# Routed attention and a feed-forward layer on one core: a second batch in cluster order, its outcome fetched by halves

## The chip, the cores and the metric

One core of a Trainium2 chip runs the whole program. The metric is the device time of one execution in microseconds, the median of three runs. A profile of one execution, taken by the hardware profiler, gives the times of single instructions.

## The reference

```python
# q, k, v: (4, 8, 768, 64); centroids: (8, 16, 64); w_in 512x2048, w_out 2048x512
q_assign = argmax(normalised(q) . normalised(centroids))      # 16 clusters per head
k_assign = argmax(normalised(k) . normalised(centroids))
mask = q_assign[:, :, :, None] == k_assign[:, :, None, :]
scores = where(mask, q @ k.T / 8, -1e9)
attn = softmax(scores) @ v                                     # (B, H, S, D)
x = attn as (B*S, H*D) = (3072, 512)
h = x @ w_in
out = (maximum(h, 0) + alpha * minimum(h, 0)) @ w_out
```

A query attends only to keys of its own cluster. Everything is in fp32.

## The kernel before

**Attention.** There are 4 batches with 4 *pairs* of heads each; a tile holds both heads of a pair, 64 partitions each. The first `WHOLE` batches (3 before) are done *whole*: for each half of the queries (384) all six chunks of 128 keys are scored on TensorE (`score`, L757), exponentiated on ScalarE (L778, L775), masked on VectorE by comparing cluster numbers (`mask`, L798; batch 0 is masked in the product instead), summed up (`add_up`, L808; `turn`, L827; `rows_sums`, L835), inverted and spread (`invert`, L861; `spread_out`, L868), weighed with v (`weigh`, L893) and normalised into `xT` (`normalise`, L993).

The other batches go in *cluster order*. `order_features` (L564), `order_sims` (L573), `order_counts`, `order_begins` (L598), `order_ranks`, `order_rows` (L619) and `order_clusters` find for each token its row in the order of clusters. `order_stage` (L652, SP) loads a third of a head's q, k and v (256 tokens) into one of two stage tiles; `order_scatter` (L663, POOL) sends 64 of these tokens to their rows in DRAM by an indirect DMA, four for each stage. These stand in the list `sorting`, 24 scatters and 6 stages a pair. Later `order_load` (L674, L683, L692, 12 DMAs on SP) fetches the ordered pair; `order_blocks` (L699) and `order_queries` (L705) on VectorE prepare it. As neighbours in order are of equal or neighbouring clusters, a chunk of keys is scored against at most three chunks of queries (`window`): 2048 columns a head where a whole pair has 4608. `add_near`, `weigh_near` (L926) and `normalise_near` (L932) end it. Then `to_rows` (L955, L958) turns the outcome to rows, `put_back` (L963, POOL) sends it by 12 indirect DMAs to the tokens' rows in DRAM, `fetch_back` (L975, SP) reads it in token order and `turn_back` (L985, VectorE) transposes it into `xT`.

**Feed-forward layer.** `ffn_pieces` makes 28 pieces for each half of a batch: 16 `hidden` (L1017, copied on ScalarE, sloped on VectorE, L1009) and 12 `final` (L1035). The last batch goes by `last_pieces` (L1195, L1251), a scheme with fewer products on halves of x and w.

**Order.** The order is written by hand (`manual_schedule`). Time is counted in steps; three steps (15 ticks, 12 of them slots) are one half of a whole pair or one ordered pair, and 12 steps one block (`UB`). A block does attention, and between it feeds pieces of the layer for the block before; `kept(block)` pieces are left for the next. `load_at` and `prep_at` hold what starts at a step; `later(ticks, piece)` defers; `ORDERS` holds the steps in which an ordered pair's raw tiles are loaded. `steps` lists the whole batches and then the ordered ones:

```python
steps += [(n, None, s) for n in range(NO, NP) for s in range(SB)]
```

Every engine runs its own instructions in this order. POOL's queue holds scatters and put-backs, SP's queue every plain load and store. Buffers by pool: `inp` 4 (raw q and k, outcome before and after it is put back), `vpool` 4, `xpool` 2 (`xT`), stage tiles 2.

Of the kernel before, what the change touches and what calls it, by code (L numbers as in the profile page):

```python
# [23 lines left out]
def kernel(  # L24
# [19 lines left out]
    HJ = NJ // 2  # L44
    HS = HJ * P
    SCALE = float(D) ** -0.5
    WHOLE = 3

    GROUP = 2
    assert D == 64 and S % (2 * P) == 0 and HS <= 512 and DM == H * D and H * NC == P  # L50
# [60 lines left out]
    def load(n):  # L111

        b, hp = pairs[n]
        for w, src in enumerate((q, k)):
            raw = inp.tile([P, 2, NJ, D], FP32, name="qk")
            if n < NCH:
                nc.sync.dma_start(
                    out=raw.rearrange("p h j d -> p h (j d)"),  # L120
                    in_=src[b, 2 * hp:2 * hp + 2].rearrange("h (p j) d -> p h (j d)",
                                                            j=NJ))
            for h in range(2):
                rows = src[b, 2 * hp + h]
# [367 lines left out]
    def second_part():  # L492

        first_part.close()
        for name, bufs in (("emore", 1), ("ordc", 1), ("ordp", 1), ("order", NP - NO),
                           ("xmore", 1), ("byrow", 1)):
            sorts[name] = fast.enter_context(tc.tile_pool(name=name, bufs=bufs))
        for i in range(5):
            e_tiles.insert(0, sorts["emore"].tile([P, 2, HS], FP32, name=f"more{i}"))
# [78 lines left out]
    def order_counts(n, ps):  # L578

        top, first, pieces = argmax(ps, exact=True)  # L580
        member = sorts["ordp"].tile([P, HS], BF16, name="mine")
        pieces.append(lambda: nc.vector.transpose(
            out=member, in_=top.rearrange("p t c -> p (t c)")))

        def scan():
            count = asg.tile([P, HS], FP32, name="simT")
            nc.vector.tensor_tensor_scan(count, member, member, 0.0, ALU.add, ALU.max)
            us[n] = member, count
        pieces.append(scan)
# [339 lines left out]
    def normalise_near(n):  # L929
        outT = inp.tile([P, 2, NJ, D], FP32, name="qk").rearrange("p h j d -> p (h j d)")  # L930
        for side in range(2):
            nc.vector.tensor_tensor(out=outT[:, side * HS:(side + 1) * HS],  # L932
                                    in0=pos.pop((n, side))[:, 0:HS],
                                    in1=rds.pop((n, side)), op=ALU.mult)
        whole = tc.dram_tile([2 * S, D], FP32, name=f"back{n}")
        to = dram_disjoint_views(whole, 2 * NJ)
        found = orders.pop(n)
        place = sorts["order"].tile([P, 2, NJ], I32, name="place")
        nc.vector.tensor_scalar(out=place, in0=found[:, :, :, 0], scalar1=0, scalar2=S - 1,
                                op0=ALU.max, op1=ALU.min)  # L940
        rows = sorts["byrow"].tile([P, NJ, P], FP32, name="rows")

        starts = (6, 9)
        for i in range(2):
            later(starts[i], lambda i=i: to_rows(outT, rows, i))
            for x in range(NJ):
                later(starts[i] + 2 + x // 2,
                      lambda i=i, x=x: put_back(to, place, rows, i * NJ + x))
        later(starts[1] + 2 + HJ, lambda: fetch_back(n, whole))

    def to_rows(outT, rows, i):

# [12 lines left out]
            out_offset=bass.IndirectOffsetOnAxis(ap=place[:, h, j:j + 1], axis=0),  # L965
            in_=rows[:, j, h * D:(h + 1) * D], in_offset=None, element_offset=h * S * D)

    def fetch_back(n, whole):

        b, hp = pairs[n]  # L970
        raw = inp.tile([P, 2, NJ, D], FP32, name="qk").rearrange("p h j d -> p (h j d)")
        for h in range(2):
            for x in range(D // Q):
                r = h * D + x * Q
                nc.sync.dma_start(  # L975
                    out=raw[r:r + Q, :].rearrange("p (t i) -> p t i", i=Q),
                    in_=whole[h * S:(h + 1) * S, x * Q:(x + 1) * Q].rearrange(
                        "(t p) i -> p t i", p=Q))

        def turn_back():  # L980
            for half in range(2):
                if (b, half) not in xTs:
                    pool = sorts["xmore"] if half else xpool
                    xTs[b, half] = pool.tile([P, NCH, HS], FP32, name="xT")
                nc.vector.transpose(out=xTs[b, half][:, hp, :],  # L985
                                    in_=raw[:, half * HS:(half + 1) * HS])
        later(4 if n == NP - 1 else 9, turn_back)

    def normalise(n, half):
        b, hp = pairs[n]  # L990
        if (b, half) not in xTs:
            xTs[b, half] = xpool.tile([P, NCH, HS], FP32, name="xT")
        nc.vector.tensor_tensor(out=xTs[b, half][:, hp, :],  # L993
                                in0=pos.pop((n, half))[:, 0:HS],
                                in1=rds.pop((n, half)), op=ALU.mult)

# [83 lines left out]
            nc.vector.tensor_tensor(out=to, in0=x, in1=y, op=op)  # L1080

    def sum_x(which):
        x0, x1 = (xTs[B - 1, half] for half in range(2))
# [5 lines left out]
        B11, B21, B12, B22 = (x0[:, 0:KH], x0[:, KH:NCH], x1[:, 0:KH], x1[:, KH:NCH])  # L1089
        for to, x, y in ((T1, B12, B11), (T2, B22, T1), (B12, B22, B12), (T4, B21, T2))[which]:  # L1090
            nc.vector.tensor_tensor(out=to, in0=x, in1=y, op=ALU.subtract)

    def last_pieces():
# [93 lines left out]
        def hidden(x):  # L1187
# [12 lines left out]
            def x_of(half, kh):  # L1200
                return xTs[b, half][:, kh * KH:(kh + 1) * KH]

            def g_of(f, half):
                return g[f][0][half]
# [1 line left out]
            def p1():  # L1206
                if not g:
                    places()
                copy(g_of(f1, 0), product("a", "11", x_of(0, 0), True))

            def p5():
                copy(g_of(f2, 1), product("e", "S1", x_sums[0], True))

            def p2():
                plus(g_of(f1, 0), product("z", "12", x_of(0, 1), True))
                if late:
                    late.popleft()()

# [1 line left out]
                copy(g_of(f1, 1), product("a", "S2", x_sums[1], False))  # L1220

            def p3():
                plus(g_of(f1, 1), product("e", "S4", x_of(1, 1), False))
                slopes(f1)

            def p7():
                plus(g_of(f2, 1), product("a", "S3", x_of(1, 0), False))
                late.append(p4)
                if x % 2 == 0 and x:
                    g_sums(x - 2)  # L1230
# [508 lines left out]
```

## Time and profile before

| | before |
|---|---|
| median of 3 runs | 968.09 us (967.7 to 968.3) |
| the profiled execution: device time / span | 968.97 / 967.2 us |
| PE (products) busy | 946.1 us, 98% |
| VectorE (DVE) busy | 683.5 us, 71% |
| ScalarE (ACT) busy | 260.0 us, 27% |
| GpSimd (POOL) busy | 213.2 us, 22% |
| TensorE clock granted | 1.0 throughout |
| 16 DMA engines busy (queue of SP) | 25.6% |

By stages (us from the start of the span; busy times of the engines in it):

| stretch | length | PE | DVE | ACT | POOL | what |
|---|---|---|---|---|---|---|
| 221 to 341 | 120 | 119.4 | 87.5 | 27.9 | 17.6 | batch 1, first half whole |
| 341 to 461 | 120 | 120.0 | 89.9 | 28.1 | 37.0 | batch 1, second half whole |
| 461 to 581 | 120 | 120.0 | 91.3 | 27.7 | 17.4 | batch 2, first half whole |
| 581 to 693 | 112 | 110.9 | 84.9 | 27.2 | 37.9 | batch 2, second half whole |
| 693 to 806 | 113 | 106.7 | 77.6 | 25.6 | 47.7 | batch 3 in cluster order |

How to read it: an instruction of an engine that works in order starts when the one before it has ended and its operands are there. An engine that is idle costs time only if what it does next is waited for by the chain that ends last. DMA-issuing instructions on POOL count as busy for the time POOL takes over them, not for the transfer.

### The profile page before, as it was taken

How to read it: one execution, taken by the hardware profiler on the slowest of the kernel's cores; microseconds unless marked ns; L12 is line 12 of the kernel's file. 1: busy time of each engine (PE TensorE's matmuls, PEld its weight loads, DVE VectorE, ACT ScalarE, POOL GpSimd, SP SyncE). 2: the span in 40 equal slices, each digit the busy share in tenths (PEclk: the TensorE clock that was granted, in tenths of full speed). 3: DMA queues.
4: the chain of work that ended last, by engine and by line, in shares of the span. 5: the costliest groups of instructions: out<-in, count | busy, mean ns of one | idle time of the engine just before them, and what ended most of it. 6: DMA issues, size and time to landing. Idle time of an engine off the chain costs nothing.

```text
span 967.2 us, 11202 instructions
## 1 busy us (share of the span) xinstructions
PE 946.1 (98%) x4059; PEld 502.8 (52%) x4059; DVE 683.5 (71%) x1241; ACT 260.0 (27%) x474; POOL 213.2 (22%) x249
## 2 busy tenths in 40 slices
PE   8999999999999999999999999999998999999997
PEld 5534444445454454544545445454454454556886
DVE  5897788798587776977868777678888735598200
ACT  5764533323121231222312223222222210121000
POOL 1432222110000645401000065550043541000000
PEclk9999999999999999999999999999999999999999
DMA  8433666053200463416020031450621112000000
GB/s 290 141 113 102 143 136 118 17 114 88 55 1 22 127 134 70 87 28 123 1 33 1 25 89 50 94 103 11 88 49 30 33 32 56 1 1 0 21 24 25
DMA packets 175583, 64.67 MB, mean 67 GB/s; under 512 B 161360, under 2 KB 165152, under 8 KB 175520
## 3 DMA queue, kind: packets, MB, share of 16 engines
q1 hardware_dynamic: 170064, 55.62, 25.6%
q0 software_dynamic: 4608, 7.87, 2.5%
q8 instruction: 34, 0.56, 0.2%
q10 hardware_dynamic: 848, 0.39, 0.2%
q14 instruction: 29, 0.24, 0.1%
HBM read 45.15 MB, written 18.35 MB: 66 GB/s over the span
## 4 chain that ended last, share of the span: by engine, by line
PE 92%; DVE 5%; issue 1%; ACT 1%; POOL 0%; DVEq 0%; ACTq 0%; POOLq 0%
PE fps L1035 25%; PE fps L1017 25%; PE vps L893 9%; PE sps L757 8%; PE sps L1251 4%; PE sps L1195 4%; PE fps L757 3%; PE vps L1251 2%; PE vps L1195 2%; PE fps L1251 1%; PE fps L1195 1%; PE mps L381 1%; PE mps L926 1%; PE vps L926 1%; PE sps L766 1%
## 5 line engine op out<-in xcount | busy, mean ns | idle before, releaser
L1017 PE MATMUL fps<-xT,w_in_sb 128*128 128x384 f32 x768 | 259.2, 491 | 0.0
L1035 PE MATMUL fps<-w_out_sb,gT 128*128 128x512 f32 x576 | 256.0, 597 | 1.1 <-DVE gT L1009 1.1
L1017 PEld LDWEIGHTS fps<-xT,w_in_sb 128*128 128x128 f32 x768 | 142.3, 190 | 103.9 <-ACT more L778 4.4
L663 POOL DMA_INDIRECT scratch<-stage,off x96 | 102.0, 1063 | 324.8 <-DMA stage<-in_v_dram 269.7
L1035 PEld LDWEIGHTS fps<-w_out_sb,gT 128*128 128x128 f32 x576 | 106.9, 190 | 127.2 <-issue 117.9
L1023 ACT COPY gT<-fps 128x384 f32<-128x384 f32 x96 | 45.9, 478 | 225.0 <-PE fps L1017 212.5
L798 DVE SCALAR_TENSOR_TENSOR more<-aq,key,more 128x384 f32<-128x384 bf16 (+1 forms) x136 | 74.5, 606 | 35.1 <-ACT more L778 20.0
L757 PE MATMUL sps<-qkT 64*128 64x384 f32 (+1 forms) x512 | 97.4, 494 | 0.1
L1009 DVE SCALAR_TENSOR_TENSOR gT<-gT,alpha 128x384 f32<-128x384 f32 x96 | 61.3, 646 | 33.2 <-ACT gT L1023 24.0
L778 ACT ACTIVATE E<-sps 128x768 f32<-128x768 f32 (+1 forms) x81 | 61.0, 801 | 73.2 <-PE sps L766 38.4
L963 POOL DMA_INDIRECT back<-rows,place x48 | 47.7, 994 | 105.1 <-ACT rows L958 91.7
L757 PEld LDWEIGHTS sps<-qkT 64*128 64x128 f32 x512 | 46.3, 186 | 45.0 <-issue 18.1
L798 DVE SCALAR_TENSOR_TENSOR E<-aq,key,E 128x384 f32<-128x384 bf16 (+1 forms) x104 | 56.6, 601 | 17.2 <-ACT E L778 11.3
L893 PE MATMUL vps<-E,vt 128*64 128x384 f32 x356 | 65.7, 494 | 1.5 <-DVE xT L993 1.5
L808 DVE TENSOR_TENSOR acc<-acc,E 128x768 f32<-128x768 f32 x47 | 44.9, 955 | 14.9 <-ACT E L778 13.6
L778 ACT ACTIVATE more<-sps 128x768 f32<-128x768 f32 (+1 forms) x47 | 35.6, 796 | 49.6 <-PE fps L1035 21.6
L893 PEld LDWEIGHTS vps<-E,vt 128*64 128x64 f32 x356 | 23.0, 136 | 33.4 <-issue 31.0
L271 POOL TENSOR_TENSOR w_in_sb<-w_in_sb,power 128x512 f32<-128x512 f32 x16 | 24.3, 1520 | 71.2 <-DVE w_in_sb L268 71.2
L893 PE MATMUL vps<-more,vt 128*64 128x384 f32 x220 | 38.8, 491 | 0.0
L1041 ACT COPY y<-fps 128x512 f32<-128x512 f32 x18 | 10.5, 586 | 100.8 <-PE fps L1035 81.6
L757 PE MATMUL fps<-qkT 64*128 64x384 f32 x160 | 34.9, 508 | 0.6 <-ACT more L775 0.6
L271 POOL TENSOR_TENSOR w_out_sb<-w_out_sb,power 128x512 f32<-128x512 f32 x16 | 22.5, 1410 | 55.8 <-DVE w_out_sb L268 55.8
(282 smaller groups left out, 1074.4 us busy)
## 6 DMA issues: line engine op xcount, KB each, us to landing
raw<-in_moe_w_in_dram SPq DMA_DIRECT2D x16, 512.0 KB
raw<-in_moe_w_out_dram SPq DMA_DIRECT2D x16, 512.0 KB
out_dram<-y SPq DMA_DIRECT2D x21, 256.0 KB
vt<-in_v_dram SPq DMA_DIRECT2D x12, 384.0 KB
qk<-in_q_dram SPq DMA_DIRECT2D x48, 96.0 KB
qk<-in_k_dram SPq DMA_DIRECT2D x48, 96.0 KB
w_in_kept<-w_in_sb SPq DMA_DIRECT2D x8, 512.0 KB
qk<-scratch SPq DMA_DIRECT2D x32, 96.0 KB
```

The costliest lines, as they stand in the source:

```text
L271: nc.gpsimd.tensor_tensor(out=dst, in0=dst, in1=power[0].bitcast(FP32), op=ALU.mult)
L663: nc.gpsimd.indirect_dma_start(out=scratch[n][1][h * NX + xx], out_offset=bass.IndirectOffsetOnAxis(ap=ranks[n][:, xx, h:h + 1], axis=0), ...
L757: nc.tensor.matmul(out=bank(ps, h, m), lhsT=qkT[r:r + D, S + c * P:S + (c + 1) * P], rhs=qkT[r:r + D, tokens], start=True, stop=not early_ ...
L778: nc.scalar.activation(out=E[:, :, 0:m], in_=ps[:, :, 0:m], func=AF.Exp, scale=SCALE)
L798: nc.vector.scalar_tensor_tensor(out=e, in0=of, scalar=keys[n][:, NJ + c, h:h + 1], in1=e, op0=ALU.is_equal, op1=ALU.mult)
L893: nc.tensor.matmul(out=po[r:r + D, 0:HS], lhsT=vts[n][:, h, c, :], rhs=e[:, h, :], start=(c == 0), stop=(c == NJ - 1))
L963: nc.gpsimd.indirect_dma_start(out=to[i], out_offset=bass.IndirectOffsetOnAxis(ap=place[:, h, j:j + 1], axis=0), in_=rows[:, j, h * D:(h + ...
L1009: nc.vector.scalar_tensor_tensor(out=gs[f], in0=gs[f], scalar=alpha[:, f:f + 1], in1=gs[f], op0=ALU.mult, op1=ALU.max)
L1017: nc.tensor.matmul(out=ps[:, 0:HS], lhsT=w_in_sb[:, c, f * P:(f + 1) * P], rhs=xTs[b, half][:, c, :], start=(c == 0), stop=(c == NCH - 1))
L1035: nc.tensor.matmul(out=ps[:, 0:DM], lhsT=gs[f][:, i * P:(i + 1) * P], rhs=w_out_sb[:, f, :], start=on and f == f0, stop=off and f == f0 + ...
L1195: nc.tensor.matmul(out=bank[to], lhsT=w_in_form(m, x, cc), rhs=rhs[:, cc, :], start=start and cc == 0, stop=cc == KH - 1, skip_group_check ...
L1251: nc.tensor.matmul(out=bank[to], lhsT=g_form(m, x, t), rhs=w_out_form(n, x), start=start and x == 0, stop=x == NQ - 1, skip_group_check=no ...
```

## The change

Batch 2 joins batch 3 in cluster order (`WHOLE = 2`), so there are 8 ordered pairs in place of 4 and 72 steps in place of 84. All eight are ordered by steps 26 to about 57, in and after batch 1; up to two entries of `sorting` a slot are done in place of one. The features are transposed in place, and their raw tiles come from a pool of their own with two buffers, `inp2`. `order_begins` follows its counts by ticks instead of at a step.

The outcome of an ordered pair of batch 2 comes back by halves of its tokens: the first half at the tick at which the whole came back so far, the second half (`inp2`) in steps 62 to 65. Batch 3 comes back behind the last block, whole. The second half of the last batch's x lies in two tiles of `inp2` (`x_last`) and no longer in a pool `xmore`. `kept` leaves 2, 4, 12 and 34 pieces after blocks 2 to 5 (before: 4 and 12 after blocks 5 and 6).

```diff
-    WHOLE = 3
+    WHOLE = 2
...
-            raw = inp.tile([P, 2, NJ, D], FP32, name="qk")
+            raw = (inp if n < NO else sorts["inp2"]).tile([P, 2, NJ, D], FP32, name="qk")
...
-        for name, bufs in (("emore", 1), ("ordc", 1), ("ordp", 1), ("order", NP - NO),
-                           ("xmore", 1), ("byrow", 1)):
+        for name, bufs in (("emore", 1), ("ordc", 1), ("ordp", 1), ("order", 5),
+                           ("inp2", 2), ("byrow", 1)):
...
     def order_features(n, w):
-        us[n, w] = inp.tile([P, 2, NJ, D], FP32, name="qk").rearrange("p h j d -> p (h j d)")
-        nc.vector.transpose(out=us[n, w],
-                            in_=raw_qk.pop((n, w)).rearrange("p h j d -> p (h j d)"))
+        us[n, w] = raw_qk.pop((n, w)).rearrange("p h j d -> p (h j d)")
+        nc.vector.transpose(out=us[n, w], in_=us[n, w])
...
+        later(len(pieces) + 3, lambda: order_begins(n))
...
-        later(starts[1] + 2 + HJ, lambda: fetch_back(n, whole))
+        backs[n] = whole
+        if pairs[n][0] < B - 1:
+            later(starts[1] + 2 + HJ, lambda: fetch_back(n, (0,)))
+        elif n == NP - 1:
+            for i in range(NCH):
+                later((1, 4, 7, starts[1] + 2 + HJ)[i],
+                      lambda i=i: fetch_back(NP - NCH + i, (0, 1)))
...
-    def fetch_back(n, whole):
+    backs, x_last = {}, []
+
+    def fetch_back(n, halves):
 
         b, hp = pairs[n]
-        raw = inp.tile([P, 2, NJ, D], FP32, name="qk").rearrange("p h j d -> p (h j d)")
+        whole = backs[n]
+        t0, t1 = halves[0] * HS, (halves[-1] + 1) * HS
+        raw = (sorts["inp2"] if halves == (1,) else inp).tile(
+            [P, 2, NJ, D], FP32, name="qk").rearrange("p h j d -> p (h j d)")
         for h in range(2):
             for x in range(D // Q):
                 r = h * D + x * Q
                 nc.sync.dma_start(
-                    out=raw[r:r + Q, :].rearrange("p (t i) -> p t i", i=Q),
-                    in_=whole[h * S:(h + 1) * S, x * Q:(x + 1) * Q].rearrange(
+                    out=raw[r:r + Q, t0:t1].rearrange("p (t i) -> p t i", i=Q),
+                    in_=whole[h * S + t0:h * S + t1, x * Q:(x + 1) * Q].rearrange(
                         "(t p) i -> p t i", p=Q))
 
         def turn_back():
-            for half in range(2):
-                if (b, half) not in xTs:
-                    pool = sorts["xmore"] if half else xpool
-                    xTs[b, half] = pool.tile([P, NCH, HS], FP32, name="xT")
-                nc.vector.transpose(out=xTs[b, half][:, hp, :],
+            for half in halves:
+                nc.vector.transpose(out=x_of(b, half, hp),
                                     in_=raw[:, half * HS:(half + 1) * HS])
         later(4 if n == NP - 1 else 9, turn_back)
 
+    def x_of(b, half, hp):
+        if (b, half) == (B - 1, 1):
+            if not x_last:
+                x_last.extend(sorts["inp2"].tile([P, 2, NJ, D], FP32, name="qk").rearrange(
+                    "p h j d -> p (h j d)").rearrange("p (c q) -> p c q", q=HS)
+                    for _ in range(2))
+            return x_last[hp // 2][:, hp % 2, :]
+        if (b, half) not in xTs:
+            xTs[b, half] = xpool.tile([P, NCH, HS], FP32, name="xT")
+        return xTs[b, half][:, hp, :]
...
-    ORDERS = [27, 33, 51, 57]
+    ORDERS = [26, 29, 33, 36, 40, 43, 46, 49]
...
-                at(t + 2, 2 + 2 * i, lambda n=n, i=i: order_features(n, i))
+                at(t + 2, 2 + i, lambda n=n, i=i: order_features(n, i))
...
-            at(t + 7, 2, lambda n=n: order_begins(n))
...
-            for i, p in ((5, 0), (7, 1)):
+            for i, p in ((-7, 0), (-5, 1)):
...
-        return {NS // UB - 2: 4, NS // UB - 1: 12}.get(block, 0)
+        return {2: 2, 3: 4, 4: 12, 5: 34}.get(block, 0)
...
+    for i in range(NCH):
+        load_at.setdefault(NS - UB + 2 + i, []).append(
+            lambda i=i: fetch_back(NO + i, (1,)))
...
-        if u == ORDERS[0] - 2:
+        if u == TOGETHER + 1:
             order_constants()
...
-            if sorting:
+            for _ in range(min(2, len(sorting))):
                 sorting.popleft()()
```

The products of the last batch read `x_last` in place of `xTs[B - 1, 1]`, with no other change.

More of the change, by code (lines that the diff above doesn't have):

```diff
@@ L975, in fetch_back @@
                 nc.sync.dma_start(
-                    out=raw[r:r + Q, :].rearrange("p (t i) -> p t i", i=Q),
-                    in_=whole[h * S:(h + 1) * S, x * Q:(x + 1) * Q].rearrange(
+                    out=raw[r:r + Q, t0:t1].rearrange("p (t i) -> p t i", i=Q),
+                    in_=whole[h * S + t0:h * S + t1, x * Q:(x + 1) * Q].rearrange(
                         "(t p) i -> p t i", p=Q))
         def turn_back():
-            for half in range(2):
-                if (b, half) not in xTs:
-                    pool = sorts["xmore"] if half else xpool
-                    xTs[b, half] = pool.tile([P, NCH, HS], FP32, name="xT")
-                nc.vector.transpose(out=xTs[b, half][:, hp, :],
+            for half in halves:
+                nc.vector.transpose(out=x_of(b, half, hp),
                                     in_=raw[:, half * HS:(half + 1) * HS])
         later(4 if n == NP - 1 else 9, turn_back)
+    def x_of(b, half, hp):
[8 more added lines that the diff above has]
+        return xTs[b, half][:, hp, :]
     def normalise(n, half):
         b, hp = pairs[n]
-        if (b, half) not in xTs:
-            xTs[b, half] = xpool.tile([P, NCH, HS], FP32, name="xT")
-        nc.vector.tensor_tensor(out=xTs[b, half][:, hp, :],
+        nc.vector.tensor_tensor(out=x_of(b, half, hp),
                                 in0=pos.pop((n, half))[:, 0:HS],
@@ L1082, in sum_x @@
     def sum_x(which):
-        x0, x1 = (xTs[B - 1, half] for half in range(2))
+        x0 = xTs[B - 1, 0]
         if not x_sums:
@@ L1088, in sum_x @@
         T1, T2, T4 = x_sums
-        B11, B21, B12, B22 = (x0[:, 0:KH], x0[:, KH:NCH], x1[:, 0:KH], x1[:, KH:NCH])
+        B11, B21, B12, B22 = (x0[:, 0:KH], x0[:, KH:NCH], *x_last)
         for to, x, y in ((T1, B12, B11), (T2, B22, T1), (B12, B22, B12), (T4, B21, T2))[which]:
@@ L1198, in product, with x_part @@
                 return bank[to]
-            def x_of(half, kh):
-                return xTs[b, half][:, kh * KH:(kh + 1) * KH]
+            def x_part(half, kh):
+                return x_last[kh] if half else xTs[b, 0][:, kh * KH:(kh + 1) * KH]
             def g_of(f, half):
@@ L1208, in p1 @@
                     places()
-                copy(g_of(f1, 0), product("a", "11", x_of(0, 0), True))
+                copy(g_of(f1, 0), product("a", "11", x_part(0, 0), True))
             def p5():
@@ L1214, in p2 @@
             def p2():
-                plus(g_of(f1, 0), product("z", "12", x_of(0, 1), True))
+                plus(g_of(f1, 0), product("z", "12", x_part(0, 1), True))
                 if late:
@@ L1222, in p3 @@
             def p3():
-                plus(g_of(f1, 1), product("e", "S4", x_of(1, 1), False))
+                plus(g_of(f1, 1), product("e", "S4", x_part(1, 1), False))
                 slopes(f1)
             def p7():
-                plus(g_of(f2, 1), product("a", "S3", x_of(1, 0), False))
+                plus(g_of(f2, 1), product("a", "S3", x_part(1, 0), False))
                 late.append(p4)
```

## Prediction

> **What bounds the kernel now.** I read the page's totals, the chain, the windows by stage, and then the timelines of POOL and SP, because the change gives work to those two. The page, engines' totals and POOL's line of the 40 slices:
>
> ```profile
> PE 946.1 (98%) x4059; PEld 502.8 (52%) x4059; DVE 683.5 (71%) x1241; ACT 260.0 (27%) x474; POOL 213.2 (22%) x249
> POOL 1432222110000645401000065550043541000000
> ```
>
> PE has 98% of the span; POOL's mean of 22% hides slices at 6 tenths. The chain that ended last, four pieces (start, us, what, instructions):
>
> ```profile
> 673.59 4.02 PE vps L893 x24
> ...
> 698.37 1.88 PE vps L926 x16
> 700.25 1.73 PE mps L926 x16
> ...
> 722.27 1.88 PE vps L926 x16
> ```
>
> The weighing of one *half* of a whole pair costs 4.02 us, that of a *whole* cluster-ordered pair 1.88 + 1.73 = 3.61 us. The windows (length, then PE, PEld, DVE, ACT, POOL busy, clock, DMA, GB/s):
>
> ```profile
> 461.00:581.00 120.00, 120.00 (x460) 59.12 (x459) 91.33 (x160) 27.65 (x52) 17.40 (x20) 1.00 0.13 30
> ...
> 698.00:722.00 24.00, 22.10 (x112) 12.66 (x108) 22.46 (x41) 6.96 (x15) 8.75 (x9) 1.00 0.38 62
> 722.00:754.60 32.60, 29.16 (x116) 14.63 (x114) 21.72 (x39) 7.33 (x14) 14.52 (x15) 1.00 0.12 29
> ```
>
> In a whole-pair block PE never rests and DVE has 76%. In the cluster-ordered block PE already loses 1.9 and 3.4 us in two pairs, and DVE has 22.46 of 24 us. POOL's timeline (start, us, line, operation, idle before and releaser):
>
> ```profile
> 370.57 0.96 POOL L663 DMA_INDIRECT scratch<-stage,off  x1 [0.30 <-issue]
> 371.84 0.96 POOL L663 DMA_INDIRECT scratch<-stage,off  x1 [0.31 <-issue]
> ...
> 630.98 1.02 POOL L663 DMA_INDIRECT scratch<-stage,off  x1 [6.14 <-DMA stage<-in_v_dram]
> ...
> 749.96 0.95 POOL L963 DMA_INDIRECT back<-rows,place  x1 [0.30 <-issue]
> 751.21 0.96 POOL L963 DMA_INDIRECT back<-rows,place  x1 [0.30 <-issue]
> ```
>
> From one start to the next a scatter (L663) takes 1.27 us, a put-back (L963) 1.27 us; the copy between scatters with its gap (374.07 to 374.54) takes 0.48. The 6.14 us are SP's doing:
>
> ```profile
> 618.47 6.17 SPq L683 DMA_DIRECT2D qk<-scratch  x8
> ```
>
> Here SP issued the loads of an ordered pair one after the other, and POOL's next stage stood behind them.
>
> **What the change removes.** Call a stretch the three steps of one score set: 1a0 to 1a3 and 1b0 to 1b3 for the two halves of batch 1, 2.0 to 2.3 and 3.0 to 3.3 for the ordered pairs. Per pair of batch 2, PE loses 8.04 - 3.61 = 4.43 us of weighing. The scores go from 4608 to 2048 columns a head; at the same 4.02 us for 12 products of 384 columns that is 8.04 x (1 - 2048/4608) = 4.47. It gains six transposes (L955, 4.1 us for four pairs, so 1.0) and two one-column products (0.2), and loses one denominator product (0.1). Net -7.8 a pair, -31.4 for four. Four stretches fewer save some 0.65 us each of small gaps (full stretches last that much longer than the sum of their products): -2.6. The 6 us that PE idled between 698 and 774 go into the account of what comes next. The span without any new wait would be 967.2 - 31.4 - 2.6 - 6 = 927.
>
> **What it adds.** Scatters go from 96 to 192, put-backs from 48 to 96, stage loads from 72 to 144, ordered loads from four pairs to eight. As the program is built, all 192 scatters stand between the end of 1a2 and the end of 3.0, and the put-backs of 2.0 to 2.3 stand in 2.1, 2.2, 2.3 and 3.0, between scatters, on the same queue. Counting instructions by the rows' durations (us; POOL = 1.27 per DMA + 0.48 per copy):
>
> | stretch | 1a3 | 1b0 | 1b1 | 1b2 | 1b3 | 2.0 | 2.1 | 2.2 | 2.3 | 3.0 | sum |
> |---|---|---|---|---|---|---|---|---|---|---|---|
> | PE | 29.8 | 26.0 | 33.1 | 23.9 | 29.0 | 25.1 | 22.3 | 27.6 | 20.6 | 30.9 | 268 |
> | DVE | 29.6 | 26.3 | 27.4 | 27.1 | 34.4 | 31.6 | 35.2 | 29.1 | 22.7 | 27.0 | 290 |
> | POOL | 27.8 | 25.3 | 26.5 | 26.0 | 27.8 | 27.8 | 40.5 | 41.8 | 41.3 | 37.5 | 322 |
>
> For example 2.1 on POOL: 18 scatters and 12 put-backs, 30 x 1.27, and 5 copies. DVE's 35.2 there is a near pair's 21 us (masks 6.8, sums, turns, blocks), some 10 us of one pair's ordering (L564 0.95 twice, argmax chain 3.1, scan 0.93, ranks, begins) and slopes. PE's work shrinks, and that of the two engines beside it grows in the same place.
>
> **Who waits for POOL.** The outcome of pair 2.k is put back in the next stretch; `fetch_back` on SP waits for its twelfth put-back (all rows may lie in either half); `turn_back` on DVE stands 9 ticks later, 40% into the stretch after, and DVE runs in order, so behind it queue masks, sums and slopes, and PE behind those. And xT of batch 2, half 0, is needed at about the same place: twelve pieces of batch 1 (36 us) are kept to cover it, and stretches 3.0 and 3.1 eat them. So POOL's 322 us must be over by 40% into 3.1. PE alone would be there 268 + 10 x 0.65 + 0.4 x 36 = 289 us after the start of 1a3.
>
> **The sum.** 1a3 begins at 290.2 in the profile, about 289 after the change (1a1 and 1a2 together are 1.7 shorter on PE). Up to the end of 1b1 POOL is paced by PE (90.9 with gaps): 380. In 1b2, 1b3 and 2.0 POOL's 81.6 exceeds PE's 78, and three ordered loads each hold SP. The two such places before cost POOL 6.14 and 1.97 us; I take 4 each: 94, so 474. In 2.1 to 3.0 POOL has 161 against PE's 101; the put-backs between scatters give the stage loads time, 4 for waits: 639. Then completion 1.5 (a scatter ended at 374.1, SP went on at 375.6), four issues 2.4 and landing 2: 645 for the last turn. PE's remaining work: 0.6 of 3.1 (21), 3.2 (37), and 3.3 with the tail, which is counted at 281 and, by the gap between count and trace in the tail before (205.6 counted, 214.7 lasted), lasts 290. That is 645 + 21 + 37 + 290 = 993. Add 1.8, which lay around the span in the profiled execution (968.97 against 967.2); the median lay 0.9 below that execution: 994. The loss is 67 us of waiting against 40 saved.
>
> Unknown are POOL's pace under doubled traffic and SP's waits. Lower bound: POOL never waits from the start of 1a3, 1.27 each: 289 + 322 + 6 + 348 = 965, median 966. Upper: each DMA at the mean of all (scatter 1.06 + 0.30, put-back 0.99 + 0.30, copy 0.34 + 0.28), which makes 1b2 to 3.0 260 instead of 243, and 6 us for each of six ordered loads: 380 + 260 + 36 + 6 + 348 = 1030. I lean to the lower pace, because it is the median of the scatters from 560 to 650 (0.98).
>
> The edits with one answer: the features are transposed in place and the raw tiles come from a pool of two (no work moved; a load waits for the ordering before it, 3 steps earlier); up to two sorting pieces a slot are counted above. The second halves of batch 2 come back from the end of 3.0 on and batch 3 behind the last block; 34 kept pieces, some 100 us of PE, cover that, where 12 did. If that cover failed it would cost some 10 us (one fetch and one turn).
>
> **The skill against the rows.** The Trainium skill, "Perfetto Trace Analysis", Identifying the Most-Contended Engine, would have the engine of highest occupancy optimised first; that is PE, and the sum would be the 927 above. The page allows for regimes with other engines in front, and the rows by stretch show one. "DMA: Bandwidth & Descriptors", Anatomy of one DMA — SWDGE (gpsimd) path, puts a fixed 2.0 us on each such DMA, mostly completion. As POOL's own time that would make an estimated 472 us of 236 DMAs and a span over 1100; the rows' 1.27 from start to start speak against reading it so.
>
> **Rivals.** *DVE alone binds (faster).* If POOL's lateness is taken up, because put-backs land earlier than I place them or PE runs on while DVE waits, what remains is DVE's excess: from 1b2 to 2.3 it has 180 us against PE's 152 with gaps, 28, some 32 with its own idle: 927 + 32 = 959, 960 as a median. For it: DVE waited only once for a fetched outcome before ("4.3 us" of L985). Against: that was with POOL at 15 us a stretch, not 41. It decides if POOL's wall time from 1a3 to the last put-back stays under some 315 us; the sum of its rows is 322.
> *POOL and SP hold each other up (still slower).* Stage loads, ordered loads and fetches share SP's queue in order, and there are only two stages: 6 us at every ordered load and the slower pace give 1010 to 1030. For it: the 6.14 us row. Against: put-backs between scatters leave the loads time.
> *Nothing to measure.* POOL at its lower bound gives 966, by chance beside 968.
>
> **How the numbers follow.** POOL sets the end with moderate waits (975 to 1010): 0.64, my forecast, 994. POOL and SP together, over 1010: 0.24. Near the lower bound, within 0.2% (966.2 to 970, about what a measurement of this kernel can tell from no change): 0.04. Faster: 0.08, the DVE rival. The range leaves out the faster case and the top of the SP case: 969 to 1020.
>
> **What would show it.** Right: POOL over 85% busy from about 380 to 640; PE idle for 60 us or more, in 1b3 to 3.1; DVE's `turn_back` (L985, after the change L993) waiting tens of us for DMA of back; SP's fetch waiting for put-backs; PE busy down to some 915. Wrong: `turn_back` waits under 10 us in all, or POOL shows gaps in 2.1 to 3.0 and PE none; then the time is below 960. If PE's idle time lies before masks while POOL has rest, DVE was the bound.

## The result and the profile after

| | before | after |
|---|---|---|
| median | 968.11 us (4 runs, 967.7 to 968.3) | 1073.78 us (4 runs, 1066.0 to 1079.9) |
| profiled execution: device time / span | 968.97 / 967.2 us | 1066.01 / 1064.2 us |
| PE idle, 290 to 760 (before: 290 to 806) | 7.4 us | 90.5 us |
| granted clock, mean | 1.0 | 0.946 |

The ratio of the medians is 1.109, with a 95% interval of 1.101 to 1.117. The loss is 106 us where 26 were forecast, and the time lies outside the range.

Page after the change, engines' totals, POOL's line and the clock's line of the 40 slices:

```profile
PE 955.7 (90%) x3931; PEld 507.3 (48%) x3931; DVE 659.8 (62%) x1229; ACT 246.0 (23%) x450; POOL 363.2 (34%) x417
POOL 2342222000271746666764756524425100000000
PEclk9999999999999899999868777989999999999999
```

PE executes 128 products fewer (3931 against 4059), and yet is busy 10 us longer, because several of the slices in which POOL works have a clock of 6 to 8 tenths. POOL itself is not full there: mostly 4 to 7 tenths. Windows after the change (length, then PE, PEld, DVE, ACT, POOL, clock, DMA, GB/s):

```profile
402.00:520.00 118.00, 103.79 (x417) 50.78 (x417) 106.98 (x199) 23.04 (x46) 80.13 (x90) 0.94 0.59 126
520.00:600.00 80.00, 50.26 (x187) 24.45 (x185) 38.23 (x72) 12.45 (x24) 49.41 (x56) 0.82 0.38 81
600.00:700.00 100.00, 69.28 (x236) 34.35 (x235) 45.79 (x83) 15.22 (x31) 62.38 (x70) 0.77 0.38 82
...
290.00:760.00 470.00, 379.52 (x1395) 186.87 (x1394) 308.45 (x561) 85.60 (x166) 270.37 (x298) 0.88 0.42 92
```

From 520 to 700 no engine is full, and the 16 DMA engines are 38% busy. What the forecast named as the wait, `turn_back` (L993), is almost absent. The view of that line gives all that VectorE waited before it:

```profile
its engine sat idle before it (us, times) until:
  DMA qk<-back: 3.1, 1
```

Instead there are stretches in which PE, VectorE and ScalarE stand still together. One of them in the timeline, the weighing of an ordered pair and the scores behind it:

```profile
598.41 0.49 ACT L775 ACTIVATE E<-fps 128x384 f32<-128x384 f32 x1 [2.33 <-remote]
599.80 0.59 PE L926 MATMUL mps<-more,vt 128*64 128x256 f32 x1 [1.68 <-issue]
602.54 0.96 POOL L663 DMA_INDIRECT scratch<-stage,off  x1 [0.30 <-issue]
603.81 0.96 POOL L663 DMA_INDIRECT scratch<-stage,off  x1 [0.30 <-issue]
604.00 0.80 PE L757 MATMUL fps<-qkT 64*128 64x384 f32 x1 [1.30 <-issue]
606.10 0.79 PE L757 MATMUL fps<-qkT 64*128 64x384 f32 x1 [1.31 <-issue]
...
617.32 0.96 POOL L663 DMA_INDIRECT scratch<-stage,off  x1 [0.30 <-issue]
620.73 0.56 DVE L932 TENSOR_TENSOR qk<-vps,rd 128x384 f32<-128x384 f32 x1 [21.17 <-remote]
620.93 0.87 ACT L775 ACTIVATE E<-fps 128x384 f32<-128x384 f32 x2 [22.02 <-remote]
...
623.64 1.13 POOL L969 DMA_INDIRECT back<-rows,place  x1 [5.36 <-ACT rows L964]
```

The last product of the weighing starts at 599.80 and needs 0.59 us. `normalise_near` (L932), which waits for it alone, starts at 620.73. In between PE starts one product in some 2.1 us, with nothing in the profile that it waits for ("issue"). POOL goes on at its 1.27 us, with one pause of 2.0 us at 611.5, and 2.4 us after its last scatter (617.32 + 0.96) VectorE and ScalarE move again. Such stretches lie at 357 to 370, 527 to 557, 594 to 621 and 643 to 664. In them PE is busy for 20 to 40% of the time, VectorE for about a tenth, and each falls into a close series of POOL's indirect DMAs.

### The profile page after: what moved, and what is told of

Same layout as the page of the kernel before. It is cut to its first block, busy times and chain, and to the rows that moved or that the text cites. A ratio compares the mean times of both kernels' runs of the same rounds, so it can differ in the third digit from the quotient of the medians.

```text
span 1064.2 us, 11465 instructions
## 1 busy us (share of the span) xinstructions
PE 955.7 (90%) x3931; PEld 507.3 (48%) x3931; DVE 659.8 (62%) x1229; ACT 246.0 (23%) x450; POOL 363.2 (34%) x417
## 4 chain that ended last, share of the span: by engine, by line
PE 70%; DVE 9%; issue 9%; another core or an unknown queue 4%; DMA 3%; POOL 2%; SPq 2%; ACT 1%; POOLq 0%; DVEq 0%; ACTq 0%
PE fps L1034 20%; PE fps L1052 19%; PE sps L757 5%; PE vps L893 4%; PE sps L1268 4%; PE sps L1212 4%; POOL scratch L663 2%; PE vps L1268 2%; PE vps L1212 2%; PE fps L757 2%; PE vps L926 1%; PE mps L926 1%; DVE acc L808 1%; PE fps L1268 1%
## 5 line engine op out<-in xcount | busy, mean ns | idle before, releaser
L1034 PE MATMUL fps<-xT,w_in_sb 128*128 128x384 f32 x768 | 270.8, 506 | 25.5 <-ACT more L775 13.1
L663 POOL DMA_INDIRECT scratch<-stage,off x192 | 197.6, 1029 | 185.2 <-DVE off L619 68.0
L969 POOL DMA_INDIRECT back<-rows,place x96 | 96.2, 1002 | 122.8 <-ACT rows L964 96.0
L798 DVE SCALAR_TENSOR_TENSOR more<-aq,key,more 128x384 f32<-128x384 bf16 (+1 forms) x110 | 59.2, 592 | 33.6 <-ACT more L778 18.3
L798 DVE SCALAR_TENSOR_TENSOR E<-aq,key,E 128x384 f32<-128x384 bf16 (+1 forms) x82 | 43.7, 584 | 37.7 <-issue 23.0
L893 PE MATMUL vps<-E,vt 128*64 128x384 f32 x272 | 50.7, 496 | 1.4 <-DVE xT L1010 1.4
L1060 DVE TENSOR_TENSOR y<-y,fps 128x512 f32<-128x512 f32 x24 | 16.4, 685 | 48.8 <-PE fps L1052 42.3
L808 DVE TENSOR_TENSOR acc<-acc,E 128x768 f32<-128x768 f32 x30 | 28.5, 952 | 14.4 <-ACT E L778 13.6
L1058 ACT COPY y<-fps 128x512 f32<-128x512 f32 x18 | 10.6, 586 | 100.9 <-PE fps L1052 89.0
L778 ACT ACTIVATE more<-sps 128x768 f32<-128x768 f32 (+1 forms) x38 | 28.4, 767 | 21.8 <-DVE first L408 7.3
L757 PEld LDWEIGHTS fps<-qkT 64*128 64x128 f32 x128 | 13.8, 195 | 35.3 <-issue 30.6
```

Source lines behind the costliest of these rows:

```text
L663: nc.gpsimd.indirect_dma_start(out=scratch[n][1][h * NX + xx], out_offset=bass.IndirectOffsetOnAxis(ap=ranks[n][:, xx, h:h + 1], axis=0), ...
L757: nc.tensor.matmul(out=bank(ps, h, m), lhsT=qkT[r:r + D, S + c * P:S + (c + 1) * P], rhs=qkT[r:r + D, tokens], start=True, stop=not early_ ...
L778: nc.scalar.activation(out=E[:, :, 0:m], in_=ps[:, :, 0:m], func=AF.Exp, scale=SCALE)
L798: nc.vector.scalar_tensor_tensor(out=e, in0=of, scalar=keys[n][:, NJ + c, h:h + 1], in1=e, op0=ALU.is_equal, op1=ALU.mult)
L893: nc.tensor.matmul(out=po[r:r + D, 0:HS], lhsT=vts[n][:, h, c, :], rhs=e[:, h, :], start=(c == 0), stop=(c == NJ - 1))
L969: nc.gpsimd.indirect_dma_start(out=to[i], out_offset=bass.IndirectOffsetOnAxis(ap=place[:, h, j:j + 1], axis=0), in_=rows[:, j, h * D:(h + ...
```

## The experiments

Theories after the result. *Trains*: an unbroken series of indirect DMAs on POOL holds up what the other engines report (the semaphore updates by which one engine tells another that its work is done). *Loads*: SP's loads in 128-byte packets do it. *Products*: the short products of the ordered pairs do it themselves. The kernel before, run beside each set, took 968.1 us (e1 to e4, chip 3), 968.8 (e5 to e8, chip 13), 963.8 (e9 to e12, chip 2) and 967.1 (e13 to e16, chip 10); ratios are against it. That the sets ran on four chips will matter below. The diffs are shortened. Where the order of the tokens is left out (e1, e3, e5, e16), the branch to the program's general path, which would then be taken, is held shut.

### Taking POOL's indirect DMAs out of the changed kernel

`e1_plain_scatters` (`e3_half_scatters`: the same for odd stages only, `if i % 2`):

```diff
-        nc.gpsimd.indirect_dma_start(out=scratch[n][1][h * NX + xx], ...)
+        if x == m - 1:
+            for w in range(2):
+                r0 = (2 * h + w) * S + part * S // PARTS
+                nc.sync.dma_start(
+                    out=scratch[n][0][r0:r0 + S // PARTS, :].rearrange("(x p) d -> p x d", p=TS),
+                    in_=sorts["stage"][i % STAGES][w * TS:(w + 1) * TS, :, :])
```

> The changed kernel, but each stage tile goes to DRAM by two plain transfers from SP in place of four indirect ones from POOL; the order is left out (every token keeps its place), all other work and the put-backs stay. Trains (POOL's unbroken series of indirect DMAs hold up what PE, VectorE and ScalarE report): the places where all three stand still are gone, at most two PE gaps over 5 us that nothing in the profile explains, clock above 0.99, 925 to 950 us. Loads (SP's many 128-byte packets do it): the stalls stay, 1040 to 1080 us, as these loads are all there. Products (the short products of the cluster-ordered scores and weighing do it themselves): stalls stay at the weighing, over 1030 us.

Measured: 984.45 us, ratio 1.015 (1.013 to 1.018). The 192 scatters as indirect DMAs cost 1073.8 - 984.5 = 89 us. Loads and products are refuted as the main cause, since both are all there. But the time lies 34 us above the range of *trains*, and "no stall" was too much: PE idles 11.3 us before scores, in the series of 12 put-backs.

> The changed kernel with every second stage tile sent by SP's plain transfers, the others by POOL's indirect ones (96 scatters in place of 192); the order is left out. Trains: series on POOL are broken into fours outside the put-backs, stalls are mostly gone, 930 to 975 us. Amount (what counts is how many indirect DMAs there are, not how close they stand): about half of the loss stays, 990 to 1020 us. Loads or products: 1040 to 1080 us.

Measured: 1030.95 us, ratio 1.064 (1.061 to 1.067): a miss for every theory. Fours with pauses (263 to 510) bring no long stall. But POOL, which now also waits for SP's transfers to leave the stage, comes late with the put-backs, and then VectorE waits 48.7 us for `back`. This kernel has two causes at once and tells little.

`e5_plain_both` is e1, and the put-backs go by SP too:

```diff
-            for x in range(NJ):
-                later(starts[i] + 2 + x // 2, lambda i=i, x=x: put_back(to, place, rows, i * NJ + x))
+            later(starts[i] + 4, lambda i=i: plain_back(whole, rows, i))
```

> The changed kernel with neither scatters nor put-backs on POOL: both go by plain transfers from SP, the order of the tokens is left out, all work of PE, VectorE and ScalarE stays. Trains (unbroken series of POOL's indirect DMAs hold up the other engines): no series, so no place where PE, VectorE and ScalarE stand still together; what remains is PE's saved work and VectorE's excess, 930 to 960 us, clock above 0.99. If stalls over 5 us remain that no wait in the profile explains, something besides the series makes them, and the time stays above 970 us.

Measured: 970.73 us, ratio 1.0019 (1.0008 to 1.0029). No stretch is left in which the three engines stand still, but the time stays above the range given. The put-backs cost 984.5 - 970.7 = 14 us. In this form, without any indirect DMA, the change gains nothing. Its window, and the waits of PE (total us, times, longest):

```profile
290.00:760.00 470.00, 441.23 (x1725) 225.00 (x1725) 348.64 (x651) 99.36 (x197) 13.41 (x45) 0.98 0.50 99
```

```profile
PE mps L968 <- ACT rows L971: 6.7, 3, 3.2
PE mps L442 <- DVE simT L402: 4.4, 2, 2.3
PE mps L968 <- DVE simT L402: 4.3, 1, 4.3
PE mps L442 <- ACT rows L971: 3.9, 4, 1.1
PE mps L857 <- DVE simT L402: 3.5, 2, 2.8
```

PE idles 28.8 us here (before: 7.4), and nearly all of it before products into `mps`. That is the one PSUM bank that the ordering, the cluster numbers, the denominators and `to_rows` share; each of them holds it until VectorE or ScalarE has read it out. Part of this is e5's own: ScalarE's copy into `rows` (L971) waits 9.5 us for SP's put-backs of the pair before.

`e16_after_same_place`, the control for the left-out order:

```diff
-        ranks[n] = off
+        ranks[n] = sorts["same_place"]        # iota: every token's own row
```

> The changed kernel with all its indirect DMAs, but every token is sent to its own place (the order is left out, as in the kernels with plain transfers). The stalls are the issue's doing, not the rows': 1060 to 1085 us, as the changed kernel. If scattered rows were needed for them: below 1000 us.

Measured: 1068.56 us, ratio 1.103 (1.099 to 1.107), within the changed kernel's range: leaving the order out changes nothing that can be told.

### Putting them into the kernel before

`e2_before_double`:

```diff
+        nc.gpsimd.indirect_dma_start(
+            out=twice[n][h * NX + xx], ...,      # a second time, into a tile nobody reads
+            in_=sorts["stage"][i % STAGES][:, x, :], in_offset=None, element_offset=h * 2 * S * P)
```

> The kernel before with a second, equal indirect DMA into a DRAM tile that nobody reads behind each of the 96 scatters. Trains: unbroken series of 16 to 32 on POOL in batches 1 and 2, PE gaps of 5 to 20 us that nothing in the profile explains, 985 to 1030 us. Loads or products: neither is changed, 966 to 973 us.

Measured: 1118.06 us, ratio 1.156 (1.153 to 1.158). The direction of *trains*, but 88 us above its range: 96 added DMAs cost 150 us. The largest series has 48, from 611 to 673, and in it (timeline, then the window):

```profile
669.70 0.96 POOL L670 DMA_INDIRECT twice<-stage,off  x1 [0.31 <-issue]
670.97 0.96 POOL L665 DMA_INDIRECT scratch<-stage,off  x1 [0.30 <-issue]
671.51 0.56 DVE L1000 TENSOR_TENSOR xT<-vps,rd 128x384 f32<-128x384 f32 x1 [46.44 <-remote]
```

```profile
610.00:675.00 65.00, 24.51 (x80) 9.04 (x78) 11.09 (x20) 2.38 (x4) 47.70 (x54) 0.66 0.25 75
```

VectorE stands still for 46 us, in a block of whole pairs, where nothing but POOL's queue was changed. The stall begins some 14 us after the start of the series (611.3; here at 625.07, 671.51 - 46.44) and lasts to its end, so in this kernel a long series costs about its length less 14 us. In the changed kernel the delay was 15 to 29 us.

`e4_before_trains` has the same 96 scatters closer together:

```diff
-            if sorting:
+            for _ in range(min(3, len(sorting))):
                 sorting.popleft()()
```

> The kernel before with up to three entries of the sorting list a slot in place of one: the same 96 scatters, but a pair's 24 follow each other in about 35 us. Trains: PE, VectorE and ScalarE stand still together once or twice in each of the four series, 5 to 15 us each, 980 to 1020 us. Amount, loads or products: the same number of everything, 965 to 972 us.

Measured: 1012.81 us, ratio 1.047 (1.044 to 1.050). With the number unchanged, standing closer costs 45 us.

### What in them it is

`e6_double_short_rows`, `e8_double_few_rows` and `e7_pool_memsets` change e2's second DMA:

```diff
-            in_=sorts["stage"][i % STAGES][:, x, :]          # e2: 128 rows of 512 bytes
+            in_=sorts["stage"][i % STAGES][:, x, 0:4]        # e6: 128 rows of 16 bytes
+            in_=sorts["stage"][i % STAGES][0:32, x, :]       # e8: 32 rows of 512 bytes
+        for _ in range(5):                                   # e7: no second DMA at all
+            nc.gpsimd.memset(sorts["idle"], 0.0)             #     128x128
```

> The kernel before with a second indirect DMA behind each of the 96 scatters, as in the doubled kernel, but of 16 bytes a row in place of 512, into a tile that nobody reads. If the number of rows (what POOL writes for each) counts: about as slow as the doubled kernel, 1080 to 1120 us. If the bytes moved count: near the undoubled one, 968 to 1010 us.

Measured: 1119.44 us, ratio 1.151 (1.144 to 1.159): the bytes do not count.

> The kernel before with a second indirect DMA behind each of the 96 scatters, but of 32 rows in place of 128 (512 bytes each). If the rows count one by one: a quarter of the doubled kernel's loss, 985 to 1020 us, and an issue on POOL of about a quarter of 0.96 us. If every indirect DMA costs the same whatever its rows: 1080 to 1120 us. If only the length of the series in time counts: by the row of its issue on POOL, between the two.

Measured: 1123.17 us, ratio 1.159 (1.155 to 1.163): nor do the rows. POOL takes 0.90 us for 32 rows where it takes 1.01 for 128 (means of the two kinds in this kernel).

> The kernel before with five fills of a 128x128 tile on POOL (some 1 us, no DMA) behind each of the 96 scatters: POOL is as long without rest as in the doubled kernel, with half of its indirect DMAs. If a busy POOL is enough: 1080 to 1120 us. If the indirect DMAs must follow each other closely: 966 to 985 us.

Measured: 968.49 us, ratio 0.9997 (0.998 to 1.001): a POOL as busy as in e2 (319.8 us; e2 303.7) harms nobody, if its indirect DMAs are some 2.4 us apart.

### How far apart

`e9_double_1_fill`, `e14_double_short_fill`, `e15_double_fill_each_4`, `e10_double_3_fills`: e2 with fills on POOL behind its indirect DMAs.

```diff
         nc.gpsimd.indirect_dma_start(...)                    # scatter, then the second one
+        nc.gpsimd.memset(sorts["idle"], 0.0)   # e9: 128x128 behind each; e14: 128x1; e15: behind
+                                               # every fourth; e10: three times behind each
```

> The doubled kernel (before, with a second equal indirect DMA behind each of the 96 scatters) with one fill of a 128x128 tile on POOL (0.25 us) behind each of the 192. If any ordinary instruction between two indirect DMAs is enough to keep the other engines free: 968 to 990 us. If it is the pace (one indirect DMA in 1.27 us is too close, one in 2.5 us is not): some 1.6 us from start to start, still most of the stalls, 1020 to 1110 us.

Measured: 964.01 us, ratio 1.0005 (0.9995 to 1.0014). The loss of 150 us is absent, with all 192 DMAs (96 scatters, each with its second one) and a POOL almost without pause from 316 to 463 and from 556 to 705.

> The doubled kernel with a fill of 128x1 (one column, the shortest there is) behind each of the 192. Pace: it adds little to the 1.27 us from start to start, so much of the loss of the doubled kernel stays, over 1020 us. Kind (any ordinary instruction between two indirect DMAs is enough): 968 to 980 us on a chip where the kernel before takes 968.

Measured: 1112.74 us, ratio 1.147 (1.141 to 1.153).

> The doubled kernel with one fill of 128x128 behind every fourth indirect DMA only. Pace: 1.34 us on average, nearly the whole loss, 1080 to 1120 us. Kind, with a series of four as harmless: 968 to 990 us. The changed kernel, whose four scatters of a stage are followed by a copy on POOL, and which stalls, speaks against the second.

Measured: 1105.12 us, ratio 1.145 (1.141 to 1.149): a fill behind every fourth does not help. POOL's timeline of e9 and the window 612 to 672 there:

```profile
636.52 0.96 POOL L666 DMA_INDIRECT scratch<-stage,off  x1 [0.17 <-issue]
637.48 0.23 POOL L672 MEMSET idle<- 128x128 f32 x1
637.88 0.96 POOL L673 DMA_INDIRECT twice<-stage,off  x1 [0.17 <-issue]
```

```profile
612.00:672.00 60.00, 59.57 (x228) 29.56 (x229) 42.70 (x72) 14.66 (x29) 52.63 (x85) 1.00 0.34 79
```

The same of e14:

```profile
634.70 0.96 POOL L666 DMA_INDIRECT scratch<-stage,off  x1 [0.19 <-issue]
635.66 0.11 POOL L672 MEMSET idle<- 128x1 f32 x1
635.96 0.96 POOL L673 DMA_INDIRECT twice<-stage,off  x1 [0.19 <-issue]
```

```profile
612.00:672.00 60.00, 33.45 (x102) 14.47 (x100) 16.11 (x28) 4.99 (x8) 45.49 (x87) 0.77 0.25 75
```

The short fill hides in the gap of 0.30 us that is there anyway: 1.26 us from start to start. With the long one it is 1.36. Read together, these runs look like a limit in the pace: by the closest distances between 1.26 and 1.36 us; by the means over whole series, with their copies and longer issues, between 33.2 / 24 = 1.38 (the changed kernel, 342 to 375, stalls) and 147.6 / 96 = 1.54 (e9, none). The result of e9 lay nearest the number given for "any ordinary instruction"; e14 and e15 speak against that theory, and if it is the pace, the expectation for e9 put the limit too high.

But that the fill took the loss away is not shown. e9 ran on chip 2; e2 ran on chip 3, e14 and e15 on chip 10, and neither e2 nor the changed kernel ran on chip 2. There are signs that chip 2 does not stall at this pace at all. The put-backs have no fill in e9 and stand 1.26 us apart as before, and at their end the kernel before has a short stall within the weighing of a pair (first two rows), e7 on chip 13 a like one (0.98 us). In e9 the same 16 products run through (third row):

```profile
723.98 1.43 PE L926 MATMUL mps<-E,vt 128*64 128x384 f32 x9
726.46 0.27 PE L926 MATMUL mps<-E,vt 128*64 128x128 f32 x1 [1.05 <-issue]
723.37 1.90 PE L938 MATMUL mps<-E,vt 128*64 128x384 f32 x16
```

In none of the four kernels on chip 2 does PE stand still for over 0.3 us with "issue" as the reason between 220 and 830, though the put-backs of e9 and e10 have no fill; and the kernel before is 3.3 to 5.1 us faster there than on the other chips. e2 on chip 2, or e9 on chip 3, would decide it. On the chips that stall, what is shown is harm at 1.26 to 1.27 us and none at 2.4 (e7).

> The same with three fills behind each of the 192, some 2.1 us from start to start. Pace: at four fifths of the distance that did no harm with 96, few stalls, 968 to 1000 us, of which up to 15 us may be POOL's own queue, which is now about 100 us a pair. If the number of indirect DMAs counts and not their distance: 1050 to 1110 us, as the doubled kernel.

Measured: 1024.52 us, ratio 1.063 (1.061 to 1.065), against my range. At 1.9 us a DMA POOL's queue is too long, and ordinary waits set the time: VectorE 25.3 us for ordered loads and 19.7 for `back`, PE 16.4 behind ScalarE's `rows`.

### The two bounds of the changed kernel, and the kernel before with fills

`e11_after_2_fills` puts two fills of 128x32 behind each scatter and put-back of the changed kernel, `e13_before_1_fill` one of 128x128 in the kernel before, `e12_before_back_fills` three behind the put-backs alone.

> The changed kernel with two fills of a 128x32 tile on POOL behind each scatter and each put-back, some 0.3 us in all. If any ordinary instruction is enough: no stalls, but POOL's queue of about 390 us between batch 1 and 3.0 then sets the end, 1030 to 1060 us, with waits of VectorE for back and of SP for put-backs in place of the stalls. If it is the pace: stalls stay, 1050 to 1110 us.

Measured: 1054.33 us, ratio 1.095 (1.093 to 1.097). Waits of it, and the window in which they lie:

```profile
DVE xT L998 <- DMA qk<-back: 100.9, 6, 32.0
ACT rows L967 <- DMA back<-rows,place: 100.0, 4, 32.7
```

```profile
522.00:702.00 180.00, 97.31 (x370) 49.46 (x370) 74.53 (x135) 22.08 (x45) 144.65 (x352) 0.79 0.39 83
```

At 1.44 us and more a DMA, on chip 2, there are no stalls without a named cause, and the wait that the prediction named is there in full: `turn_back` (L998 here) waits 100.9 us for `back`. Beside it stands one that the prediction missed: there is a single buffer `rows`, and ScalarE's copy into it waits in order until the put-backs of the pair before have left POOL's queue.

> The kernel before with one fill of a 128x128 tile on POOL behind each of its 96 scatters and 48 put-backs. If the fill frees the other engines there too, the few us that PE idles in the cluster-ordered block go: 0.2 to 0.5 per cent below the kernel before. If those waits have other causes, or the put-backs' later end (12 x 0.3 us) costs as much: within 0.2 per cent.

Measured: 965.83 us, ratio 0.9984 (0.9974 to 0.9995). In the cluster-ordered block (709 to 806) PE is busy 93.4 us, where before it is 90.7. This is the only version with an interval wholly below the kernel before, by 0.16%, a little under what was expected. It has no PE gap marked "issue" of over 0.3 us either (220 to 830), and it ran on chip 10, where e14 and e16 stall: some support for 1.36 us, but in series of 16 at most. Its 93.4 us need not come from the fills, as e9 has 93.6 there without fills behind its put-backs.

> The kernel before with three fills of a 128x128 tile behind each of the 48 put-backs, 2.1 us from start to start in place of 1.27; the scatters stay as they are. Pace: the short stall at 723 us goes, and the slow clock after it; the outcome is put back 8 us later, for which there is room: 962 to 969 us. If the short stalls are not of this kind: 967 to 972 us.

Measured: 975.76 us, ratio 1.012 (1.011 to 1.014). Both ranges are missed. Three fills are too many: the put-backs end so late that VectorE waits 25.6 us for `back`. The slow clock that the expectation speaks of is not in the trace of before (1.00 from 709 to 806).

## Why the prediction was wrong

**Direction and first terms: right.** PE's products fell to 3931, scatters stand at 192 and put-backs at 96, and most of POOL's rows have the durations taken (0.96 + 0.30).

**The step that failed** is in "what it adds": POOL's 322 us were costed as a queue that harms only those who wait for its data. The price of 1.27 us was right, but I took the pace as free. In the kernel before, the series were 4 to 16 long with pauses, and their harm was at most the 6 us that PE idled; I booked these as waits for VectorE. The change makes close series of 24, 40, 28 and 28, and in them PE, VectorE and ScalarE stand still, which no term of the sum allowed for. The loss splits so: scatters 89 us (after less e1), put-backs 14 (e1 less e5, on two chips), the rest 2 to 3 (e5 against before).

**A sign that I passed over** was in the trace of before: POOL's put-backs from 711 to 727, and in them PE with 13.7 of 16 us while VectorE too had rest. A pair of engines that idle together while a third works was the thing to ask about.

**"POOL over 85% busy, `turn_back` waiting tens of us": wrong as written** (mostly 4 to 7 tenths busy, and a wait of 3.1 us), presumably since the stalls slow PE, VectorE and ScalarE enough that POOL keeps up. The text said that such a profile would mean a time below 960; it did not, because it had no case in which PE's idle time has no releaser. Where the stalls are absent (e11) the forecast mechanism appears. The tail is nearly as summed: the forecast has 348 us behind the last turn at 645; in e11 that turn starts at 706.9 and the span ends at 1050, 343 later. What was off there is the time before it: POOL needs 420 us from 282 to 702 where the forecast had 350 (289 to 639). Some 40 of these 70 are the fills (an estimate: 240 DMAs at 1.44 in place of 1.27 us), and among the rest is the wait for the single `rows`.

**"The span without any new wait, 927" and the rival "DVE alone binds", 960.** With POOL out of the way e5 takes 970.7. The rival's size, 32 us, is near (PE idles 28.8), but the place is not DVE's sum of work: it is the shared bank `mps`. The clock, 0.989 in e5, makes up at most another 969.5 x 0.011 = 11 us (an estimate: all of it, if PE were never idle at the lower clock). Its result is that of the rival "nothing to measure", for another reason than given.

**Busy time of PE** was to fall to some 915; it rose to 955.7. Of the 95 us between the profiled executions of e5 and after (971.3 and 1066.0), 90.5 - 28.8 = 62 us are PE's idle time and 955.7 - 923.2 = 33 us the same products at a lower clock. The Trainium skill, "TensorE: Matmul & The Clock Gate", The HAM clock gate, says that an idle window of about 3.4 us brings half the clock. The ten drops granted here before the end are to half and last 3.4 us or multiples of it, as that would have it. Five of them, 89 of their 113 us, begin in the stretches named above; those at 287, 482, 506, 513 and 700 do not, and in the 3.4 us before a drop PE was busy for anything from 0 to 75% (the latter before 649.2), so "idle" is not to be read as wholly idle.

**Open.** What a close series of indirect DMAs occupies, so that the other engines stop, was not isolated. That it is neither bytes nor rows (e6, e8), nor POOL's occupation (e7), is shown. Nor is it the load on the 16 DMA engines, which are 24% busy in the 46 us of e2 and 30% from 599.6 to 620.7 after the change. Nor is it the loading of instructions: its two queues start no transfer between 586.0 and 622.8, and the engines go on at 620.7. For reports being held back, rather than the products, there is the trace's list of semaphore updates: from 598.4 to 620.7 it has none by PE, though four products that make one end there (at 600.4, 604.8, 609.0 and 617.3), and then five within 0.3 us. This is support and no proof, since the list has gaps: 521 of 595 updates by PE after the change, 561 of 605 before, while e5 and the four runs on chip 2 lack none, not even e12, whose scatters stand as in the kernel before. So indirect DMAs and the recording touch each other on the chips that stall. Every run on record comes with a span and a clock of its own; whether the stalls need the recording is not shown.

## What to carry to other kernels

Before adding work to a queue that has rest, look at how close its DMAs will stand, not only at the sum of their times: a queue's price holds for the spacing at which it was measured. When several engines idle together and the profile names no releaser, look for the engine that goes on, thin out its series or take it away, and see whether the idle time goes, with the untreated kernel beside it on the same chip. Then ask the second question at once: with the stall gone, does the change gain anything (here e5: no)?

## What the runs showed of the hardware

While POOL issues indirect DMAs 1.26 to 1.27 us apart (medians of a series), PE, VectorE and ScalarE come to a stop, in most series some 14 to 29 us after its start, for up to 52 us at a time (e6), until the series ends or up to 8 us longer (the changed kernel; e2 on chip 3, e6 and e8 on chip 13, e14 on chip 10; in e8 the pace is partly 1.16 us). At 2.4 us apart none of it is seen (e7, chip 13). With a fill of 128x128 (0.22 us) behind each, at 1.36 us and more (1.54 on average), none is seen in 96 in a row (e9), but on chip 2, where nothing was seen to stall. It does not depend on their rows (32 or 128) or bytes (16 or 512 a row). A fill of 128x1 (0.11 us) behind each does not change the distance and does not help (e14).
